# Chunked attention beside a dense expert network: scores in four row tiles, state product in one instruction, state update in column tiles

## The chip, the cores and the metric

One core of one Trainium2 chip, everything in fp32. The metric is the device time of one execution in microseconds (us).

## The reference, cut to what matters

A state-space attention over 4 sequences of 768 tokens with 8 heads (head size 32, state size 16), then a network of 4 experts (256 to 1024 to 256) over all 3072 tokens, weighted by gates.

```python
for c in range(nc):                       # chunks of one sequence
    M = einsum('bhin,bhjn->bhij', Cc, Bc) * L            # scores times decay
    y = einsum('bhij,bhjd->bhid', M, xc)                 # outputs within the chunk
      + einsum('bhin,bhnd->bhid', Cc, state) * decay_to_i  # state product
    state = decay_full * state + sum(Bc x xc * decay_from_j)  # state update
for e in range(E):
    out += p[:, e] * (maximum(x @ w1[e], 0) @ w2[e])
```

The kernel uses chunks of 128 tokens: 24 chunks, six a sequence.

## The kernel before

The expert network runs in 48 steps, each seven first-layer products (`fmul`, into the PSUM banks X and Y, a Strassen-like scheme) and seven second-layer products (`smul`, into four accumulator banks). Chunks 0 to 3 come before step 0. Each of the 20 others is woven into two steps: decays and scores in an even one, outputs and state in the odd one after it. Eight steps make a block of 512 tokens; in the step after a block (step 8, 16 and so on, here a "block end") VectorE and GpSimd combine its accumulators. Between the layers VectorE makes z from X's and Y's products, then h and the differences hT of the second layer ("subtractions" below). Eight PSUM banks are all in use: two for attention ("att"), X, Y, and four accumulators.

```python
def decays(c):                     # VectorE scans, then GpSimd
    LT  = scan(...)                # decay between tokens, by head
    bdec = B * LT[:, :, P-1:P]     # GpSimd reads LT's last column
    cts  = C * dec                 # GpSimd
def scores(c):
    for r in range(2):             # two row tiles of 64, 512 columns each
        k = slice(64 * r, 64 * r + 64)
        g = ps_att.tile([P, NH // 2, P], FP32, tag="att")
        nc.tensor.matmul(out=g, lhsT=xb[k, OBT:OBT + P], rhs=ctm[k], tile_position=(64 * r, 0))
def masked(c):                     # VectorE, in place: LT = g * LT
    for r in range(2): nc.vector.tensor_mul(LT[:, h], g[r], LT[:, h])
def added(c, ...):                 # state update: one product of 256 columns
    nc.tensor.matmul(out=A, lhsT=bdec, rhs=xb[:, 0:DM])
def outputs(c, ...):
    for t in range(NT):            # state product: two of 128 columns
        nc.tensor.matmul(out=y[:, t], lhsT=S[:, t], rhs=cts)
    ...                            # eight outputs, column tiles of 32
# one step n of the loop (cut):
load_weights(n + 2); sum_weights(n + 2)      # GpSimd adds up weights, steps 0 to 5 only
fmul 1, 2; decays(c); smul 1; fmul 6; masks(c); smul 3   # smul: those of step n - 1
outputs(c); added(c)                         # odd steps
fmul 5, 7; smul 7, 5; carry(c); smul 6; fmul 3, 4; combine 0, 1   # combine: block ends only
scores(c); smul 2, 4; masked(c)
```

`masked` overwrites LT, so it has to wait until GpSimd's bdec has read LT. GpSimd takes its work in order, and in steps 0 to 5 bdec stands behind the eight weight sums of that step.

Of the kernel before, what the change touches and what calls it, by code (L numbers as in the profile page):

```python
# [8 lines left out]
FP32 = mybir.dt.float32  # L9
AF = mybir.ActivationFunctionType  # L10
ALU = mybir.AluOpType

P = 128
NQ, NT = 4, 2
# [3 lines left out]
def kernel(  # L18
# [32 lines left out]
    nc = tc.nc  # L51

    NCH, _, W = xbc.shape
    E, DM, F = w1.shape
    NH = NQ * NT
    HN = P
    BLK = 512
    HB = BLK // 2
# [3 lines left out]
    OB, OBT, OCT = DM, DM + HN, DM + 2 * HN  # L62
# [107 lines left out]
    tmask = const.tile([P, NT], FP32, name="tmask")  # L170
    nc.vector.memset(tmask, 0.0)

    smask = const.tile([P, NT, P], FP32, name="smask")
    nc.vector.memset(smask, 0.0)
    for q in range(NQ):
        r = slice(32 * q, 32 * q + 32)
        nc.vector.memset(tmask[32 * q:32 * q + N, 0:1], 1.0)
        nc.vector.memset(smask[r, :, r], 1.0)
    nc.vector.tensor_scalar(out=tmask[:, 1:2], in0=tmask[:, 0:1], scalar1=-1.0, scalar2=1.0,
                            op0=ALU.mult, op1=ALU.add)  # L180
    for t in range(NT):
        nc.vector.tensor_scalar_mul(smask[:, t], smask[:, t], tmask[:, t:t + 1])

    cmask = const.tile([P, NQ // 2, NT], FP32, name="cmask")
    nc.vector.memset(cmask, 0.0)
    for q in range(NQ):
        r = slice(32 * q, 32 * q + 32)
        nc.vector.tensor_copy(cmask[r, q % 2], tmask[r])

    def clip(v):  # L190
        nc.vector.tensor_scalar(out=v, in0=v, scalar1=1e-6, scalar2=1.0, op0=ALU.max, op1=ALU.min)
# [33 lines left out]
    def decays(c):  # L225
        s = st[c]
        if c < DIRECT:
            clip(s["ab"])
            nc.vector.memset(s["ab"].rearrange("p (h s) -> p h s", h=NH)[:, :, 0:1], 0.0)

        LT = att.tile([P, NH * P], FP32, tag="LT", name="LT")
        nc.vector.tensor_tensor_scan(  # L232
            out=LT, data0=s["ab"], data1=ident.rearrange("p h s -> p (h s)"), initial=0.0,
            op0=ALU.mult, op1=ALU.add)
        s["LT"] = LT.rearrange("p (h s) -> p h s", h=NH)

        if c < DIRECT:
            clip(s["ah"])

        s["dec"] = dec = att.tile([HN, P], FP32, tag="dec", name="dec")  # L240
        nc.vector.tensor_tensor_scan(
            out=dec, data0=s["ah"], data1=zeros, initial=1.0, op0=ALU.mult, op1=ALU.add)
        s["bdec"] = bdec = att.tile([P, NH, N], FP32, tag="bdec", name="bdec")
        nc.gpsimd.tensor_mul(  # L244
            bdec, s["xb"][:, OB:OB + HN].rearrange("p (h n) -> p h n", h=NH),
            s["LT"][:, :, P - 1:P].to_broadcast([P, NH, N]))
        s["cts"] = cts = att.tile([HN, P], FP32, tag="cts", name="cts")
        nc.gpsimd.tensor_mul(cts, s["xb"][:, OCT:OCT + P], dec)

    def masks(c):  # L250

        s = st[c]
        m = s["ctm"] = att.tile([P, NQ // 2, NT, P], FP32, tag="ctm", name="ctm")
        for q in range(NQ // 2):
            for t in range(NT):
                nc.scalar.mul(m[:, q, t], s["xb"][:, OCT:OCT + P], cmask[:, q, t:t + 1])  # L256

    def scores(c):
        s = st[c]
        s["g"] = []  # L260
        for r in range(2):
            k = slice(64 * r, 64 * r + 64)
            g = ps_att.tile([P, NH // 2, P], FP32, tag="att", name="g")
            nc.tensor.matmul(  # L264
                out=g.rearrange("p h s -> p (h s)"), lhsT=s["xb"][k, OBT:OBT + P],
                rhs=s["ctm"][k].rearrange("p q t s -> p (q t s)"),
                start=True, stop=True, tile_position=(64 * r, 0))
            s["g"].append(g)

    def masked(c):  # L270
        s = st[c]
        for r in range(2):
            h = slice(NH // 2 * r, NH // 2 * r + NH // 2)
            nc.vector.tensor_mul(s["LT"][:, h], s["g"][r], s["LT"][:, h])  # L274

    state = {}

    def added(c, pool, tag):

        s = st[c]  # L280
        if c % chunks_per_seq < chunks_per_seq - 1:
            A = s["A"] = pool.tile([HN, NT, P], FP32, tag=tag, name="A")
            nc.tensor.matmul(  # L283
                out=A.rearrange("p t m -> p (t m)"), lhsT=s["bdec"].rearrange("p h n -> p (h n)"),
                rhs=s["xb"][:, 0:DM], start=True, stop=True)

    def outputs(c, pool, tag):
        s = st[c]
        first = c % chunks_per_seq == 0
        xb, MT = s["xb"], s["LT"]  # L290
        y = pool.tile([P, NT, P], FP32, tag=tag, name="y")
        if not first:
            for t in range(NT):
                nc.tensor.matmul(out=y[:, t], lhsT=state["S"][:, t], rhs=s["cts"],  # L294
                                 start=(t == 0), stop=False, skip_group_check=True)
        for t in range(NT):
            for q in range(NQ):
                h = NQ * t + q
                nc.tensor.matmul(  # L299
                    out=y[32 * q:32 * q + 32, t], lhsT=xb[:, h * D:h * D + D],  # L300
                    rhs=MT[:, NT * q + t], start=(first and t == 0), stop=True,
                    tile_position=(0, 32 * q), skip_group_check=True)
        k, i = divmod(c, CPB)
        if i == 0:
            yT[k] = ffn.tile([P, NT, BLK], FP32, tag="yT", name="yT")
        nc.scalar.copy(out=yT[k][:, :, i * P:i * P + P], in_=y)

    def carry(c):
        s = st.pop(c)
        if "A" not in s:  # L310
            return
        S = att.tile([HN, NT, P], FP32, tag="S", name="S")
        nc.vector.tensor_mul(S, s["A"], smask)
        if c % chunks_per_seq:
            nc.vector.scalar_tensor_tensor(
                out=S, in0=state["S"], scalar=s["dec"][:, P - 1:P], in1=S,
                op0=ALU.mult, op1=ALU.add)
        state["S"] = S

    def sums(k):  # L320

# [49 lines left out]
    def diff(n, o, x, y):  # L371
        h = hid[n]
        h[o] = ffn.tile([P, JJ, HB], FP32, tag="h" + o, name="h" + o)
        nc.vector.tensor_sub(h[o], h[x], h[y])  # L374
# [3 lines left out]
    def smul(n, i):  # L378

        if n < 0:  # L380
            return
        k = n // SPB
        u, half = divmod(ORDER.index(i), 2)
        if n % SPB == 0 and half == 0:
            acc[k, u] = ps_s.tile([P, 2, HB], FP32, tag=f"acc{u}", name=f"acc{u}")
        w = (A11, A12, S4, A22, S1, S2, S3)[i - 1]
        rhs = hid[n][("11", "21", "22", "T4", "T1", "T2", "T3")[i - 1]]
        for j in range(JJ):
            nc.tensor.matmul(  # L389
                out=acc[k, u][:, half], lhsT=w2_op(n, w)[:, j], rhs=rhs[:, j],  # L390
                start=(n % SPB == 0 and half == 0 and j == 0),
                stop=(n % SPB == SPB - 1 and j == JJ - 1), skip_group_check=True)
# [39 lines left out]

    for c in range(CPB):
        masks(c)
        scores(c)
        decays(c)
        added(c, ps_f, "X")
        masked(c)
        outputs(c, ps_f, "Y")
        carry(c)  # L440
        if c == 0:
            load_decays(1, nc.sync)
            sum_weights(0)
        if c == 1:
            gates()
            sum_weights(1)
        if c == 2:
            load_gate(0, 0)
        load_chunk(c + 2)
# [3 lines left out]
    for n in range(NS + 1):  # L453
# [6 lines left out]
        if run:  # L460
# [9 lines left out]
            total(n, 1, "11")  # L470
            gated(n, "11", "z11")
        if more and not odd:
            decays(c)
        if r == 1 and k > 0:
            leave(k - 1, 0, BLK, both)
        smul(n - 1, 1)
        if run:
            fmul(n, 6)
            snap(n, 6)
        if more and not odd:  # L480
            masks(c)
        smul(n - 1, 3)
        if ending:
            keep(k - 1, 0)
# [14 lines left out]
        if more and odd:  # L499
            carry(c)  # L500
            if c + 2 < NCH:
                load_chunk(c + 2)
        smul(n - 1, 6)
        if ending and not run:
            combine(k - 1, 0, nc.vector)
            combine(k - 1, 1, nc.vector)
            leave(k - 1, HB, HB, (nc.sync, nc.scalar))
        if run:
            fmul(n, 3)
            total(n, 6, "12")  # L510
            fmul(n, 4)
            gated(n, "21", "X")
            gated(n, "12", "z12")
            if more and r == SPB - 1:
                sums(k + 1)
            if ending:
                combine(k - 1, 0, nc.gpsimd)
                combine(k - 1, 1, nc.gpsimd)
            diff(n, "T3", "22", "12")
            diff(n, "T1", "12", "11")  # L520
        if more and not odd:
            scores(c)
        smul(n - 1, 2)
        smul(n - 1, 4)
        if run:
            diff(n, "T2", "22", "T1")
            diff(n, "T4", "21", "T2")
        if more and not odd:
            masked(c)
        if ending:  # L530
            combine(k - 1, 2, nc.vector)
            if not run:
# [46 lines left out]
```

## Time and profile before

Time before: 696.34 us, median of 3 runs (695.63 to 697.55). What each part of a chunk costs on TensorE, and the lines it is read from, stand in the prediction below. "Cost" there and here is the distance from the start of one group of matmuls to the next one's.

An fp32 matmul shows as two records. Starts are used because a matmul's end is modelled: the durations in the lines (1.03 for a group that costs 0.86) contain the drain that overlaps the next group. In a timeline line the columns are start, duration, engine, source line, operation, output and inputs, shapes, number of records, and in brackets the idle time before it with what ended it.

### The profile page before, as it was taken

Reading aid. Unit: us, or ns where it says so; the run is one execution under the profiler, and the core shown is the slowest. Engines: PE = TensorE matmul, PEld = TensorE weight load, DVE = VectorE, ACT = ScalarE, POOL = GpSimd, SP = SyncE. Lnnn points to the kernel's source line nnn. Section 1 sums busy time; section 2 is a strip of 40 time slices with the busy share of each in tenths; the row PEclk is TensorE's granted clock in tenths of the full one; section 3 lists DMA queues with packets and bytes.
Section 4 is the critical chain, followed back from the end, with each engine's and each line's share of the span. In section 5 each row is a group of like instructions: output and inputs, shape, how many; then the busy total and the mean of one; then the engine's idle time right before and its main releaser. Section 6 shows DMA issues by size and latency. Waiting matters only on the chain.

```text
span 695.9 us, 8664 instructions
## 1 busy us (share of the span) xinstructions
PE 661.2 (95%) x3289; PEld 548.2 (79%) x3289; DVE 498.5 (72%) x742; ACT 129.7 (19%) x278; POOL 110.4 (16%) x161
## 2 busy tenths in 40 slices
PE   3588999999999999999999999999999999999995
PEld 1367888887888887888887888887888888788884
DVE  5785867777865868767669858658877685765754
ACT  2120221221221112212212211212122121111110
POOL 5645847002000003000003000000200000200000
PEclk9998999999999999999999999999999999999999
DMA  8778578745655463665455664653673453563301
GB/s 295 285 240 313 171 261 296 279 151 137 237 216 174 140 236 116 205 213 210 137 177 178 174 235 159 227 174 120 181 271 125 130 208 116 142 207 135 106 1 30
DMA packets 71481, 128.89 MB, mean 185 GB/s; under 512 B 29072, under 2 KB 53008, under 8 KB 71440
## 3 DMA queue, kind: packets, MB, share of 16 engines
q1 hardware_dynamic: 66232, 112.93, 48.5%
q0 software_dynamic: 2304, 14.68, 5.3%
q10 hardware_dynamic: 2904, 0.72, 0.5%
q8 instruction: 26, 0.43, 0.3%
q14 instruction: 15, 0.12, 0.1%
HBM read 110.25 MB, written 18.07 MB: 184 GB/s over the span
## 4 chain that ended last, share of the span: by engine, by line
PE 85%; DVE 6%; POOL 1%; DMA 1%; issue 1%; SPq 0%; DVEq 0%; POOLq 0%
PE acc L389 39%; PE X L345 22%; PE Y L345 17%; PE g L264 2%; DVE h L367 2%; PE y L299 2%; PE A L283 2%; DVE hT L374 1%; DMA wt<-in_w_dram 1%; PE y L294 1%; DVE z L357 0%; DVE LT L232 0%; DVE u L409 0%; DVE yS L326 0%; POOL wt L145 0%
## 5 line engine op out<-in xcount | busy, mean ns | idle before, releaser
L357 DVE TENSOR_TENSOR z<-Y,snap 128x512 f32<-128x512 f32 x144 | 98.9, 687 | 158.3 <-ACT snap L352 106.9
L389 PE MATMUL acc<-hT,wt 128*128 128x256 f32 x768 | 181.4, 379 | 0.0
L352 ACT COPY snap<-X 128x512 f32<-128x512 f32 x144 | 84.3, 585 | 482.6 <-PE X L345 474.6
L389 PEld LDWEIGHTS acc<-hT,wt 128*128 128x128 f32 x768 | 146.0, 190 | 19.9
L389 PE MATMUL acc<-h,wt 128*128 128x256 f32 x576 | 149.9, 383 | 4.9 <-DVE u L409 4.9
L345 PE MATMUL X<-yS,wt 128*128 128x256 f32 x576 | 148.6, 381 | 0.0
L389 PEld LDWEIGHTS acc<-h,wt 128*128 128x128 f32 x576 | 107.7, 190 | 34.2 <-issue 11.4
L345 PEld LDWEIGHTS X<-yS,wt 128*128 128x128 f32 x576 | 109.9, 191 | 15.3 <-ACT snap L352 0.2
L367 DVE SCALAR_TENSOR_TENSOR h<-z,gate 128x512 f32<-128x512 f32 x144 | 101.4, 704 | 3.3
L345 PE MATMUL Y<-yT,wt 128*128 128x256 f32 x384 | 98.7, 379 | 1.8 <-DVE z L357 1.8
L345 PEld LDWEIGHTS Y<-yT,wt 128*128 128x128 f32 x384 | 72.9, 190 | 12.1 <-DVE z L357 2.2
L244 POOL TENSOR_TENSOR bdec<-xb,LT 128x128 f32<-128x128 f32 x24 | 10.3, 430 | 408.3 <-PE X L345 264.3
L374 DVE TENSOR_TENSOR hT<-h,hT 128x512 f32<-128x512 f32 x96 | 71.8, 748 | 3.3
L374 DVE TENSOR_TENSOR hT<-h,h 128x512 f32<-128x512 f32 x96 | 67.1, 740 | 1.3
L232 DVE TENSOR_TENSOR_SCAN LT<-ab,ident 128x1024 f32<-128x1024 f32 x24 | 55.9, 2328 | 4.1 <-DMA ab<-acut_d 3.9
L345 PE MATMUL Y<-yS,wt 128*128 128x256 f32 x192 | 51.2, 390 | 0.3
L345 PE MATMUL X<-yT,wt 128*128 128x256 f32 x192 | 49.5, 380 | 0.0
L264 PE MATMUL g<-ctm,xb 64*128 64x512 f32 x96 | 30.9, 724 | 13.8 <-ACT ctm L256 13.8
L345 PEld LDWEIGHTS Y<-yS,wt 128*128 128x128 f32 x192 | 36.2, 193 | 8.1 <-DVE z L357 2.6
L345 PEld LDWEIGHTS X<-yT,wt 128*128 128x128 f32 x192 | 36.3, 190 | 5.8 <-DVE h L367 0.8
L367 DVE SCALAR_TENSOR_TENSOR h<-X,gate 128x512 f32<-128x512 f32 x48 | 33.2, 691 | 8.3 <-PE X L345 8.3
L274 DVE TENSOR_TENSOR LT<-g,LT 128x512 f32<-128x512 f32 x48 | 30.7, 681 | 7.1 <-POOL bdec L244 4.0
(66 smaller groups left out, 298.2 us busy)
## 6 DMA issues: line engine op xcount, KB each, us to landing
wt<-w_d SPq DMA_DIRECT2D x80, 896.0 KB, 4.9
w_d<-wt POOLq DMA_DIRECT2D x16, 896.0 KB, 7.7
ab<-acut_d SPq DMA_DIRECT2D x23, 512.0 KB, 8.2
wt<-in_w_dram SPq DMA_DIRECT2D x32, 256.0 KB, 4.2
xb<-in_xbc_dram SPq DMA_DIRECT2D x24, 320.0 KB, 7.2
gate<-p_d SPq DMA_DIRECT2D x24, 256.0 KB, 6.8
out_dram<-ot SPq DMA_DIRECT2D x40, 64.0 KB, 2.0
ah<-ac_d SPq DMA_DIRECT2D x23, 64.0 KB
```

The lines of the kernel that those rows point to most:

```text
L232: nc.vector.tensor_tensor_scan(out=LT, data0=s["ab"], data1=ident.rearrange("p h s -> p (h s)"), initial=0.0, op0=ALU.mult, op1=ALU.add)
L244: nc.gpsimd.tensor_mul(bdec, s["xb"][:, OB:OB + HN].rearrange("p (h n) -> p h n", h=NH), s["LT"][:, :, P - 1:P].to_broadcast([P, NH, N]))
L264: nc.tensor.matmul(out=g.rearrange("p h s -> p (h s)"), lhsT=s["xb"][k, OBT:OBT + P], rhs=s["ctm"][k].rearrange("p q t s -> p (q t s)"), s ...
L274: nc.vector.tensor_mul(s["LT"][:, h], s["g"][r], s["LT"][:, h])
L283: nc.tensor.matmul(out=A.rearrange("p t m -> p (t m)"), lhsT=s["bdec"].rearrange("p h n -> p (h n)"), rhs=s["xb"][:, 0:DM], start=True, st ...
L299: nc.tensor.matmul(out=y[32 * q:32 * q + 32, t], lhsT=xb[:, h * D:h * D + D], rhs=MT[:, NT * q + t], start=(first and t == 0), stop=True, ...
L345: nc.tensor.matmul(out=f[bank][:, j], lhsT=wt1[n][:, w, j * P:j * P + P], rhs=rhs, start=(i in (1, 2, 5) and j == 0), stop=(j == JJ - 1), ...
L352: nc.scalar.copy(out=s, in_=first[n]["X"])
L357: nc.vector.tensor_add(z, first[n]["Y"], first[n][i])
L367: nc.vector.scalar_tensor_tensor(out=h, in0=first[n][src], scalar=0.0, in1=g.unsqueeze(1).to_broadcast([P, JJ, HB]), op0=ALU.max, op1=ALU. ...
L374: nc.vector.tensor_sub(h[o], h[x], h[y])
L389: nc.tensor.matmul(out=acc[k, u][:, half], lhsT=w2_op(n, w)[:, j], rhs=rhs[:, j], start=(n % SPB == 0 and half == 0 and j == 0), stop=(n % ...
```

## The change

Intent: use more of the array at once in the small attention products. Scores in four row tiles of 32, each in a PSUM bank of its own, so X and Y are borrowed for two of them (before step 0, where four chunks are done in a row, the four accumulator banks are). The state product as one of 256 columns, with C masked instead of the state. The state update in four column tiles, only the blocks that are needed. To free X and Y in time the order of a step changes too: product 6 moves behind the last first-layer product, the scores move behind product 2, and VectorE takes X's and Y's scores first.

```diff
-        for r in range(2):
-            k = slice(64 * r, 64 * r + 64)
-            g = ps_att.tile([P, NH // 2, P], FP32, tag="att", name="g")
+        for q, (pool, tag) in enumerate(homes):
+            k = slice(32 * q, 32 * q + 32)
+            g = pool.tile([P, NT, P], FP32, tag=tag, name="g")
 ...
-            A = s["A"] = pool.tile([HN, NT, P], FP32, tag=tag, name="A")
-            nc.tensor.matmul(out=A..., lhsT=s["bdec"]..., rhs=s["xb"][:, 0:DM], ...)
+            for q in range(NQ):
+                nc.tensor.matmul(out=A[32 * q:32 * q + 32], lhsT=bdec[:, 32 * q:32 * q + 32],
+                    rhs=x[:, q], start=True, stop=True, tile_position=(0, 32 * q))
 ...
-            for t in range(NT):
-                nc.tensor.matmul(out=y[:, t], lhsT=state["S"][:, t], rhs=s["cts"], ...)
+            nc.tensor.matmul(out=y, lhsT=state["M"], rhs=s["cts"], start=True, stop=False, ...)
 ...   (masks: two ScalarE products a chunk, not four; cts on GpSimd twice as wide;
 ...    carry on VectorE: three operations of 32 columns and one of 128)
-        smul(n - 1, 6)
         if run:
             fmul(n, 3) ... fmul(n, 4) ... gated(n, "21", "X") ... gated(n, "12", "z12")
+        smul(n - 1, 6)
+        if ending: combine(k - 1, 0, nc.vector) ...
             diff(n, "T3", "22", "12")
-            diff(n, "T1", "12", "11")
-        scores(c)
-        smul(n - 1, 2)
-        smul(n - 1, 4)
+        smul(n - 1, 2)
+        scores(c, ((ps_att, "att"), (ps_att, "att"), (ps_f, "X"), (ps_f, "Y")))
+        masked(c, (2, 3, 0, 1))
+        smul(n - 1, 4)
+        diff(n, "T1", "12", "11")
             diff(n, "T2", "22", "T1"); diff(n, "T4", "21", "T2")
-        masked(c)
```

More of the change, by code (lines that the diff above doesn't have):

```diff
@@ L171 @@
     nc.vector.memset(tmask, 0.0)
-    smask = const.tile([P, NT, P], FP32, name="smask")
-    nc.vector.memset(smask, 0.0)
+    qmask = const.tile([P, NQ, D], FP32, name="qmask")
+    nc.vector.memset(qmask, 0.0)
     for q in range(NQ):
@@ L177 @@
         nc.vector.memset(tmask[32 * q:32 * q + N, 0:1], 1.0)
-        nc.vector.memset(smask[r, :, r], 1.0)
+        nc.vector.memset(qmask[r, q], 1.0)
     nc.vector.tensor_scalar(out=tmask[:, 1:2], in0=tmask[:, 0:1], scalar1=-1.0, scalar2=1.0,
                             op0=ALU.mult, op1=ALU.add)
-    for t in range(NT):
-        nc.vector.tensor_scalar_mul(smask[:, t], smask[:, t], tmask[:, t:t + 1])
-    cmask = const.tile([P, NQ // 2, NT], FP32, name="cmask")
-    nc.vector.memset(cmask, 0.0)
-    for q in range(NQ):
-        r = slice(32 * q, 32 * q + 32)
-        nc.vector.tensor_copy(cmask[r, q % 2], tmask[r])
     def clip(v):
@@ L246, in decays, with scores, masked @@
             s["LT"][:, :, P - 1:P].to_broadcast([P, NH, N]))
-        s["cts"] = cts = att.tile([HN, P], FP32, tag="cts", name="cts")
-        nc.gpsimd.tensor_mul(cts, s["xb"][:, OCT:OCT + P], dec)
+        s["cts"] = cts = att.tile([HN, NT, P], FP32, tag="cts", name="cts")
+        nc.gpsimd.tensor_mul(cts, s["ctm"], dec.unsqueeze(1).to_broadcast([HN, NT, P]))
     def masks(c):
         s = st[c]
-        m = s["ctm"] = att.tile([P, NQ // 2, NT, P], FP32, tag="ctm", name="ctm")
-        for q in range(NQ // 2):
-            for t in range(NT):
-                nc.scalar.mul(m[:, q, t], s["xb"][:, OCT:OCT + P], cmask[:, q, t:t + 1])
-    def scores(c):
+        m = s["ctm"] = att.tile([HN, NT, P], FP32, tag="ctm", name="ctm")
+        for t in range(NT):
+            nc.scalar.mul(m[:, t], s["xb"][:, OCT:OCT + P], tmask[:, t:t + 1])
+    def scores(c, homes):
         s = st[c]
         s["g"] = []
-        for r in range(2):
-            k = slice(64 * r, 64 * r + 64)
-            g = ps_att.tile([P, NH // 2, P], FP32, tag="att", name="g")
+        for q, (pool, tag) in enumerate(homes):
+            k = slice(32 * q, 32 * q + 32)
+            g = pool.tile([P, NT, P], FP32, tag=tag, name="g")
             nc.tensor.matmul(
-                out=g.rearrange("p h s -> p (h s)"), lhsT=s["xb"][k, OBT:OBT + P],
-                rhs=s["ctm"][k].rearrange("p q t s -> p (q t s)"),
-                start=True, stop=True, tile_position=(64 * r, 0))
+                out=g.rearrange("p t s -> p (t s)"), lhsT=s["xb"][k, OBT:OBT + P],
+                rhs=s["ctm"][k].rearrange("p t s -> p (t s)"),
+                start=True, stop=True, tile_position=(32 * q, 0))
             s["g"].append(g)
-    def masked(c):
+    def masked(c, qs):
         s = st[c]
-        for r in range(2):
-            h = slice(NH // 2 * r, NH // 2 * r + NH // 2)
-            nc.vector.tensor_mul(s["LT"][:, h], s["g"][r], s["LT"][:, h])
+        for q in qs:
+            h = slice(NT * q, NT * q + NT)
+            nc.vector.tensor_mul(s["LT"][:, h], s["g"][q], s["LT"][:, h])
     state = {}
@@ L281, in added @@
         if c % chunks_per_seq < chunks_per_seq - 1:
-            A = s["A"] = pool.tile([HN, NT, P], FP32, tag=tag, name="A")
-            nc.tensor.matmul(
-                out=A.rearrange("p t m -> p (t m)"), lhsT=s["bdec"].rearrange("p h n -> p (h n)"),
-                rhs=s["xb"][:, 0:DM], start=True, stop=True)
+            A = s["A"] = pool.tile([HN, NT, D], FP32, tag=tag, name="A")
+            x = s["xb"][:, 0:DM].rearrange("p (t q d) -> p q t d", t=NT, q=NQ)
+            for q in range(NQ):
+                nc.tensor.matmul(
+                    out=A[32 * q:32 * q + 32],
+                    lhsT=s["bdec"].rearrange("p h n -> p (h n)")[:, 32 * q:32 * q + 32],
+                    rhs=x[:, q], start=True, stop=True, tile_position=(0, 32 * q))
     def outputs(c, pool, tag):
@@ L292, in outputs @@
         if not first:
-            for t in range(NT):
-                nc.tensor.matmul(out=y[:, t], lhsT=state["S"][:, t], rhs=s["cts"],
-                                 start=(t == 0), stop=False, skip_group_check=True)
+            nc.tensor.matmul(
+                out=y.rearrange("p t s -> p (t s)"), lhsT=state["M"].rearrange("p q d -> p (q d)"),
+                rhs=s["cts"].rearrange("p t s -> p (t s)"), start=True, stop=False,
+                skip_group_check=True)
         for t in range(NT):
@@ L311, in carry @@
             return
-        S = att.tile([HN, NT, P], FP32, tag="S", name="S")
-        nc.vector.tensor_mul(S, s["A"], smask)
+        A = s["A"]
+        S = att.tile([HN, NT, D], FP32, tag="S", name="S")
+        nc.vector.tensor_scalar_mul(S[:, 0], A[:, 0], tmask[:, 0:1])
         if c % chunks_per_seq:
             nc.vector.scalar_tensor_tensor(
-                out=S, in0=state["S"], scalar=s["dec"][:, P - 1:P], in1=S,
+                out=S[:, 0], in0=state["S"][:, 1], scalar=s["dec"][:, P - 1:P], in1=S[:, 0],
                 op0=ALU.mult, op1=ALU.add)
-        state["S"] = S
+        nc.vector.scalar_tensor_tensor(
+            out=S[:, 1], in0=A[:, 1], scalar=tmask[:, 1:2], in1=S[:, 0],
+            op0=ALU.mult, op1=ALU.add)
+        M = att.tile([HN, NQ, D], FP32, tag="M", name="M")
+        nc.vector.tensor_mul(M, S[:, 1:2].to_broadcast([HN, NQ, D]), qmask)
+        state["S"], state["M"] = S, M
     def sums(k):
@@ L434 @@
         masks(c)
-        scores(c)
+        scores(c, [(ps_s, f"acc{q}") for q in range(NQ)])
         decays(c)
         added(c, ps_f, "X")
-        masked(c)
+        masked(c, range(NQ))
         outputs(c, ps_f, "Y")
@@ L472 @@
         if more and not odd:
+            masks(c)
             decays(c)
@@ L479 @@
             snap(n, 6)
-        if more and not odd:
-            masks(c)
         smul(n - 1, 3)
@@ L502 @@
                 load_chunk(c + 2)
-        smul(n - 1, 6)
-        if ending and not run:
-            combine(k - 1, 0, nc.vector)
-            combine(k - 1, 1, nc.vector)
-            leave(k - 1, HB, HB, (nc.sync, nc.scalar))
         if run:
@@ L515 @@
                 sums(k + 1)
-            if ending:
-                combine(k - 1, 0, nc.gpsimd)
-                combine(k - 1, 1, nc.gpsimd)
+        smul(n - 1, 6)
+        if ending:
+            combine(k - 1, 0, nc.vector)
+            combine(k - 1, 1, nc.gpsimd if run else nc.vector)
+            if not run:
+                leave(k - 1, HB, HB, (nc.sync, nc.scalar))
+        if run:
             diff(n, "T3", "22", "12")
-            diff(n, "T1", "12", "11")
+        smul(n - 1, 2)
         if more and not odd:
-            scores(c)
-        smul(n - 1, 2)
+            scores(c, ((ps_att, "att"), (ps_att, "att"), (ps_f, "X"), (ps_f, "Y")))
+            masked(c, (2, 3, 0, 1))
         smul(n - 1, 4)
         if run:
+            diff(n, "T1", "12", "11")
             diff(n, "T2", "22", "T1")
             diff(n, "T4", "21", "T2")
-        if more and not odd:
-            masked(c)
         if ending:
```

## The prediction

> **What bounds the kernel now.** I read the page first: the busy line, then the chain that ended last.
>
> ```profile
> PE 661.2 (95%) x3289; PEld 548.2 (79%) x3289; DVE 498.5 (72%) x742; ACT 129.7 (19%) x278; POOL 110.4 (16%) x161
> PE 85%; DVE 6%; POOL 1%; DMA 1%; issue 1%; SPq 0%; DVEq 0%; POOLq 0%
> ```
>
> TensorE is the bound: 95% busy, 85% of the chain. VectorE at 72% has room on average. Next the chain in order of time, to see what a step costs (48 steps of the expert network, two of which carry one of 20 attention chunks; the first 4 chunks come before step 0).
>
> ```profile
> 305.63 2.59 PE acc L389 x12
> 317.71 2.59 PE acc L389 x12
> 332.70 2.59 PE acc L389 x12
> 344.79 2.59 PE acc L389 x12
> ```
>
> The same three products of successive steps: 12.08 us without attention work in between, 14.99 with a chunk's work between, 12.09 again. The plain step is 56 records at 0.216 us (12.09), so TensorE streams without a hole, and a full chunk costs 14.99 - 12.09 = 2.90 us of TensorE. This says that nearly everything the change saves on TensorE there comes off the time. The timeline of TensorE for one such pair of steps splits the 2.90:
>
> ```profile
> 321.00 1.03 PE L345 MATMUL X<-yS,wt 128*128 128x256 f32 x4
> 321.96 1.13 PE L264 MATMUL g<-ctm,xb 64*128 64x512 f32 x4
> 323.02 1.13 PE L389 MATMUL acc<-h,wt 128*128 128x256 f32 x4
> 323.99 1.03 PE L389 MATMUL acc<-hT,wt 128*128 128x256 f32 x4
> ...
> 329.17 0.61 PE L294 MATMUL y<-cts,S 128*128 128x128 f32 x4
> 329.70 0.64 PE L299 MATMUL y<-LT,xb 128*32 128x128 f32 x16
> 330.28 0.70 PE L283 MATMUL A<-xb,bdec 128*128 128x256 f32 x2
> 330.81 1.03 PE L345 MATMUL Y<-yS,wt 128*128 128x256 f32 x4
> 331.68 1.03 PE L345 MATMUL X<-yS,wt 128*128 128x256 f32 x4
> ```
>
> I read starts, since ends are modelled and overlap. A group of 4 ordinary records takes 0.86. The group before the scores takes 0.96, the scores 1.06, the group after them 0.97: together 1.06 + 0.10 + 0.11 = 1.27 for the scores. State product 0.53, outputs 0.58, state update 0.53. Sum 2.91, as above. The matmuls are fp32, two records each.
>
> **Where it is not a pure stream.** The timeline of the early steps, where GpSimd is still summing weights:
>
> ```profile
> 46.81 1.13 PE L264 MATMUL g<-ctm,xb 64*128 64x512 f32 x4
> 47.87 1.13 PE L345 MATMUL X<-yT,wt 128*128 128x256 f32 x4
> 47.97 1.18 POOL L144 TENSOR_TENSOR wt<-wt 128x256 f32<-128x256 f32 x1
> ...
> 53.64 0.42 POOL L244 TENSOR_TENSOR bdec<-xb,LT 128x128 f32<-128x128 f32 x1
> ...
> 54.10 1.29 DVE L274 TENSOR_TENSOR LT<-g,LT 128x512 f32<-128x512 f32 x2 [0.99 <-POOL bdec L244]
> ...
> 54.94 1.19 PE L294 MATMUL y<-cts,S 128*128 128x128 f32 x4 [2.48 <-DVE LT L274]
> ```
>
> The scores of step 0 are ready near 47.9, but VectorE may only multiply them into LT after GpSimd has read LT's last column (bdec), and bdec stands behind the weight sums until 53.64. Today only the outputs at 54.94 wait for that; the next step's X product starts at 47.87 untroubled. And one place at each block's end:
>
> ```profile
> 266.56 1.03 PE L345 MATMUL X<-yS,wt 128*128 128x256 f32 x4
> 267.52 1.13 PE L264 MATMUL g<-ctm,xb 64*128 64x512 f32 x4
> 269.31 1.13 PE L389 MATMUL acc<-h,wt 128*128 128x256 f32 x4 [0.66 <-DVE u L409]
> ```
>
> There the scores partly fill a wait for VectorE's combine.
>
> **What the Trainium skill says.** TensorEngine Tiling (Array Packing), Key Properties: changing the tiling mode drains TensorE. The trace agrees: about 0.10 us more on each side of the scores, and 0.10 on leaving the column-tiled outputs. Same page, Gotcha 1: row tiles must go to different PSUM banks; hence four banks, two of them X and Y. TensorE: Matmul & The Clock Gate, Part 1: after an idle window of some 3.4 us the clock halves and needs as much busy time to recover. The trace has the halving even after 2.48 us of waiting: the groups at 58.09 and 59.80 take 1.71 and 1.61 instead of 0.86. GPSIMD Engine Reference, Specifications: its SBUF interfaces contend with VectorE instructions with two SBUF inputs. Trace: a weight sum is 0.72 us alone and 1.05 to 1.18 beside VectorE's hT subtractions.
>
> **The change, part by part.**
>
> Scores: two row tiles of 64 with 512 columns become four of 32 with 256. Today's 1.06 is two passes of 512 columns at 0.43 (two tiles at once) plus 0.20. Four tiles at once are two passes at 0.216, so 0.43 + 0.20; the switches stay. Saved 0.43 a chunk. Of 20 chunks, one is in the disturbed step 0 and four in block-end steps (below): 15 x 0.43 = 6.5 us.
>
> State product: 4 records of 128 columns become 2 of 256: the same 512 columns. 0.53 is 0.43 of streaming plus the 0.10 switch into column tiling, which stays. Saved 0.
>
> State update: 2 records of 256 columns over the full array become 8 of 64 in four column tiles. Before: 0.43 + 0.10 for the switch back. After: it follows the outputs in the same mode. Streaming is two passes of 64 columns, 0.11; but the outputs' 16 records went by at 0.43/16 = 27 ns each, and I take that as the pace of short records: 8 x 27 ns = 0.22, plus the switch 0.10. Saved 0.53 - 0.32 = 0.21; 16 of the 20 chunks have an update: 3.4 us.
>
> Block ends: product 6 of the second layer moves behind the last first-layer product. In the four block ends with scores, 1.79 (267.52 to 269.31) was scores plus wait. Now product 6 (0.86) fills the 1.89 from the X group's nominal end (267.42) to 269.31, leaving 1.03 idle, then scores without cover: about nothing gained. In the last block end but one, without scores, the wait shrinks by 0.86. In all five the first-layer Y product lost 0.32 to a late z (a group of 1.09, then 0.97); earlier X ends take it away, though the third product now has one group less of slack before it and may give it back. Together 0.9 to 2.5, I take 1.7.
>
> Other engines: masked scores are 4 x 0.42 (the 128x256 from PSUM is 417 ns in the state group) instead of 2 x 0.68: +0.3. State: 2 large operations (0.42 + 0.48) become 3 of 32 columns and one of 128, an estimate of 0.7. ScalarE: 2 mask multiplications less, 0.39 each. GpSimd: cts doubles, 0.49 to about 0.9. All beside TensorE in the steady part; before step 0 the second cts delays the weight sums: +0.3.
>
> X and Y as homes of scores: in a steady step the X product of the next step stands one group (0.86) after the scores. VectorE has finished h21, h12 and T3 by then (3.0 us after the last X product starts, the scores end at 3.4), takes bank X first (0.42, to about 4.0), and X is wanted at 4.4. No wait. But in steps 0, 2 and 4 bdec is late. Step 0: bdec ends 54.06 before. VectorE now stands still instead of running its subtractions, so four weight sums go from 1.05-1.18 to 0.72-0.8: bdec about 1.5 earlier, 52.5; X free at 53.0. Five groups must then run: 4.3 us, plus 1.9 to 3.2 for a cold clock after 5 us idle, then state, outputs, update 1.35: the Y product that started at 58.09 starts about 61, but warm (it lost 1.6 to the cold clock before). Lost 1.5. Step 2: bdec ended at 81.58, X would be wanted near 81.2: with 0.42 for the bank and earlier sums, 0.4. Step 4: bdec ended at 109.36, X wanted near 107.8: about 1.3.
>
> Sum: -6.5 - 3.4 - 1.7 + 0.3 + 1.5 + 0.4 + 1.3 = -8.1. 696.3 - 8.1 = 688.2; I say 688.
>
> **The rivals.** (1) Streaming pays in full and the early steps cost nothing, because the sums finish earlier than I think: 684 to 685. For: the X wait in step 2 is within a fraction of a us. Against: in step 0 bdec is over 4 us late. (2) The new X wait becomes the story: cold clock after each of three waits (today 2.48 us was enough for it), each giving back 2 to 3 us: 692 to 696, perhaps "nothing gained". For: the cold clock in the trace; against: 1.83 us of waiting at 43 to 45 us left the next groups at 0.97. (3) The third product of each step, one group earlier, waits for VectorE's z in every step: at 316.69 the second-last X product starts, z22 ends at 319.06, and the third product would be due at 316.69 + 2.59 = 319.28. The slack is 0.2; if it is gone, 48 x 0.1 to 0.3 is 5 to 14 us: 693 to 702. (4) Four row tiles do not overlap fully: each chunk saves 0.2 less, 4 us: 692.
>
> **Range and chances.** The gains are measured terms (8 to 13); the losses (0 to 9) are guesses of order. 684 to 694 should hold it 8 times in 10. 2% faster is 682.4, below rival 1: 0.07. Slower by 2% is 710, beyond rival 3: 0.02. Within: 0.91.
>
> **What would show it.** Scores at 0.6 to 0.65 between starts instead of 1.06; state update 0.2 to 0.3; the steady pair of steps 26.4 instead of 27.08. In step 0, X waits for VectorE's masked LT for some 5 us with a clock near half behind it; short X waits near 80 and 107. Third Y product: a z wait in most steps would prove rival 3. If the four scores take 0.8 or more, rival 4. I am wrong if steady steps gain under 0.4, or if early steps lose over 6 us.

## The result, and the profile after

688.79 us, median of 4 runs (688.62 to 690.81), against 695.99 before (695.47 to 697.55, 4 runs): ratio 0.990, 95% interval 0.9875 to 0.9924. Ratios here and below are the mean time of one kernel's runs over that of the other's of the same rounds, so they are not quite the ratio of the quoted medians. Predicted: 688, within 684 to 694. The interval of 0.75 to 1.25% lies wholly below the 2% mark. All outputs are right.

The page of the changed kernel, its busy line and its chain by engine:

```profile
PE 644.4 (94%) x3465; PEld 539.0 (78%) x3465; DVE 500.4 (73%) x823; ACT 116.1 (17%) x230; POOL 112.4 (16%) x161
PE 88%; DVE 3%; DMA 2%; POOL 1%; issue 0%; SPq 0%; DVEq 0%; POOLq 0%
```

TensorE lost 17 us of busy time, and the time fell by 7 to 9: not all of the saving arrived. Where it did, the timeline of the changed kernel shows it (the pair of steps that answers to 321 to 332 us before):

```profile
320.83 1.03 PE L392 MATMUL acc<-h,wt 128*128 128x256 f32 x4
321.78 0.71 PE L256 MATMUL g<-ctm,xb 32*128 32x256 f32 x8
322.43 1.13 PE L392 MATMUL acc<-hT,wt 128*128 128x256 f32 x4
322.64 1.42 DVE L266 TENSOR_TENSOR LT<-g,LT 128x256 f32<-128x256 f32 x4 [0.47 <-PE g L256]
323.39 1.03 PE L348 MATMUL X<-yT,wt 128*128 128x256 f32 x4
...
327.71 0.59 PE L288 MATMUL y<-cts,M 128*128 128x256 f32 x2
328.24 0.64 PE L295 MATMUL y<-LT,xb 128*32 128x128 f32 x16
328.70 0.29 PE L277 MATMUL A<-xb,bdec 128*32 128x64 f32 x8
328.92 1.13 PE L348 MATMUL Y<-yS,wt 128*128 128x256 f32 x4
329.89 1.03 PE L348 MATMUL X<-yS,wt 128*128 128x256 f32 x4
```

The scores cost 0.65 (321.78 to 322.43) instead of 1.06. State product 0.53, as before. Outputs and update together 0.68 (328.24 to 328.92) plus 0.11 on the group after, 0.79; before it was 0.58 + 0.53 = 1.11. X starts at 323.39, exactly 0.96 after the group before it: no wait, though VectorE began on the scores only at 322.64.

Where it did not, in the early steps:

```profile
49.04 0.70 PE L256 MATMUL g<-ctm,xb 32*128 32x256 f32 x4 [0.15 <-DVE h L370]
...
53.85 0.42 POOL L236 TENSOR_TENSOR bdec<-xb,LT 128x128 f32<-128x128 f32 x1
54.31 1.42 DVE L266 TENSOR_TENSOR LT<-g,LT 128x256 f32<-128x256 f32 x4 [3.60 <-POOL bdec L236]
54.79 2.07 PE L348 MATMUL X<-yT,wt 128*128 128x256 f32 x4 [5.05 <-DVE LT L266]
56.66 1.84 PE L348 MATMUL Y<-yT,wt 128*128 128x256 f32 x4
...
111.39 1.13 PE L348 MATMUL X<-yT,wt 128*128 128x256 f32 x4 [1.61 <-DVE LT L266]
```

The scores of step 0 are done near 49.7, bdec ends at 54.27, VectorE multiplies, and only then X is free: 5.05 us of idle TensorE. The two groups after it start 1.87 and 1.68 apart instead of 0.86: the clock has halved. X waited another 1.61 us at 111.39, in step 4.

Step 0 also opens at half pace, before any scores of its own. Its first two products, after and then before:

```profile
38.02 2.07 PE L348 MATMUL X<-yT,wt 128*128 128x256 f32 x4
39.89 1.70 PE L348 MATMUL Y<-yT,wt 128*128 128x256 f32 x4
```

```profile
38.21 1.13 PE L345 MATMUL X<-yT,wt 128*128 128x256 f32 x4
39.17 1.03 PE L345 MATMUL Y<-yT,wt 128*128 128x256 f32 x4
```

The third product starts at 41.42 and at 40.04, so the two cost 3.40 us after and 1.83 before. In the one profile that each kernel has, the nine kernels with four-tile scores before step 0 (the changed one and runs 1, 4, 5 and 8 to 12) take 2.36 to 3.57 for these two products, and the five with two-tile scores 1.83 to 2.00. Why the full pace comes back later is not shown by any run.

The same by steps. A step's length is the distance between its first X product and the next step's, read from TensorE's timeline in each profile:

| profile | start of step 0 | steps 0 and 1 | steps 2 to 5 | steps 6 to 47 with the tail |
|---|---|---|---|---|
| before | 38.21 | 29.24 | 53.27 | 575.15 |
| after | 38.02 | 31.99 | 54.44 | 562.49 |
| difference | -0.19 | +2.75 | +1.17 | -12.66 |

From step 6 on the change is worth 12.7 us. The early steps take back 3.7. Of the 2.75 in steps 0 and 1, 1.57 lie in the opening of step 0, and 1.18 behind the start of its scores (21.83 us from there to step 2, against 20.64).

### The profile page after: what moved, and what is told of

The parts are those of the page before. It is cut to its first block, busy times and chain, and to the rows that moved or that the text cites. A ratio compares the mean times of both kernels' runs of the same rounds, so it can differ in the third digit from the quotient of the medians.

```text
span 687.0 us, 9082 instructions
## 1 busy us (share of the span) xinstructions
PE 644.4 (94%) x3465; PEld 539.0 (78%) x3465; DVE 500.4 (73%) x823; ACT 116.1 (17%) x230; POOL 112.4 (16%) x161
## 4 chain that ended last, share of the span: by engine, by line
PE 88%; DVE 3%; DMA 2%; POOL 1%; issue 0%; SPq 0%; DVEq 0%; POOLq 0%
PE acc L392 41%; PE X L348 24%; PE Y L348 18%; DMA wt<-in_w_dram 2%; PE g L256 2%; PE y L295 2%; DVE h L370 1%; PE y L288 1%; DVE LT L224 1%; DVE LT L266 0%; DVE u L412 0%; POOL wt L145 0%; POOL wt L144 0%; PE A L277 0%; POOL wt L146 0%
## 5 line engine op out<-in xcount | busy, mean ns | idle before, releaser
L392 PE MATMUL acc<-hT,wt 128*128 128x256 f32 x768 | 191.1, 382 | 0.0
L392 PEld LDWEIGHTS acc<-hT,wt 128*128 128x128 f32 x768 | 144.3, 190 | 25.2 <-issue 6.3
L392 PE MATMUL acc<-h,wt 128*128 128x256 f32 x576 | 148.3, 380 | 4.9 <-DVE u L412 4.9
L348 PE MATMUL Y<-yT,wt 128*128 128x256 f32 x384 | 100.2, 384 | 2.0 <-DVE z L360 2.0
L377 DVE TENSOR_TENSOR hT<-h,hT 128x512 f32<-128x512 f32 x96 | 68.9, 718 | 3.3
L377 DVE TENSOR_TENSOR hT<-h,h 128x512 f32<-128x512 f32 x96 | 65.0, 701 | 1.3
L348 PE MATMUL X<-yT,wt 128*128 128x256 f32 x192 | 51.5, 392 | 6.7 <-DVE LT L266 6.7
L266 DVE TENSOR_TENSOR LT<-g,LT 128x256 f32<-128x256 f32 x96 | 34.0, 416 | 20.9 <-PE g L256 12.3
L348 PEld LDWEIGHTS Y<-yS,wt 128*128 128x128 f32 x192 | 34.7, 189 | 6.5 <-issue 0.8
L256 PE MATMUL g<-ctm,xb 32*128 32x256 f32 x192 | 19.9, 473 | 11.6 <-ACT ctm L247 11.5
```

The lines of the kernel that those rows point to most:

```text
L256: nc.tensor.matmul(out=g.rearrange("p t s -> p (t s)"), lhsT=s["xb"][k, OBT:OBT + P], rhs=s["ctm"][k].rearrange("p t s -> p (t s)"), start ...
L266: nc.vector.tensor_mul(s["LT"][:, h], s["g"][q], s["LT"][:, h])
L348: nc.tensor.matmul(out=f[bank][:, j], lhsT=wt1[n][:, w, j * P:j * P + P], rhs=rhs, start=(i in (1, 2, 5) and j == 0), stop=(j == JJ - 1), ...
L377: nc.vector.tensor_sub(h[o], h[x], h[y])
L392: nc.tensor.matmul(out=acc[k, u][:, half], lhsT=w2_op(n, w)[:, j], rhs=rhs[:, j], start=(n % SPB == 0 and half == 0 and j == 0), stop=(n % ...
```

## The experiments

In each profile a step's difference from its neighbour kernel can be read to 0.01 us from step 6 on; before that, steps vary with the clock and with when bdec is done.

**1. Weight sums behind bdec, in the changed kernel.** The theory: a late bdec holds bank X, now a home of scores. So let GpSimd do bdec first.

```diff
             load_weights(n + 2)
-            sum_weights(n + 2)
 ...
         decays(c)
+    if run and n + 2 < NS:
+        sum_weights(n + 2)
```

> The changed kernel with one thing moved: in each step GpSimd sums the weights of two steps ahead after the chunk's bdec and cts, not before them. Theory (bank X, now a home of scores, is held by a late bdec): the X waits of 5.0 us in step 0 and 1.6 us in step 4 vanish, and with the first the cold clock behind it (1.8 us); steps 0 and 1 together fall from 32.0 to about 24.2 us and step 4 from 14.7 to about 12.95: some 9 us less, 680 us. Rival (the early steps lose because the prologue ends later and the clock is in another phase, or the weights come late): the waits move to another releaser and the time stays at 687 or above.

Measured: 682.61 us (681.78 to 684.46), ratio to before 0.9805 (0.9784 to 0.9825). Step 4 went from 14.70 to 12.93 as expected, its X wait was gone. Steps 0 and 1 came to 27.91, not 24.2: a shorter X wait stayed in step 0, and the slow clock with it; the opening at half pace (2.93 us for two products) stayed too.

```profile
51.80 2.07 PE L348 MATMUL X<-yT,wt 128*128 128x256 f32 x4 [1.70 <-DVE LT L266]
53.67 1.57 PE L348 MATMUL Y<-yT,wt 128*128 128x256 f32 x4
```

The reason of the wait is in the order of the step: in step 0 there is no previous step, so products 6, 2 and 4 of the second layer are missing, and with them the 2.6 us in which VectorE otherwise gets to the scores. The theory holds in direction; 6.2 us of the expected 9 came.

**2. The same move in the kernel before.**

```diff
             load_weights(n + 2)
-            sum_weights(n + 2)
 ...
         decays(c)
+    if run and n + 2 < NS:
+        sum_weights(n + 2)
```

> The kernel before with the same move of the weight sums. Here no scores lie in X, so only the wait of the outputs of 2.5 us in step 1 and the cold clock behind it (3.1 us) can go: about 5.5 us less, 690.5 us. Together with the run of the changed kernel with this move it tells the change's worth without the early wait: theory, 10 to 11 us instead of 7.2. Rival (the early waits cost both kernels alike): again about 7.

Measured: 694.55 (693.72 to 696.44), ratio 0.9976 (0.9956 to 0.9997). Step 1 fell by 3.9, but in this profile step 0 began 1.2 later, and little was left. Together with run 1, on the same chip and rounds: 0.9805 / 0.9976 = 0.983. With the weight sums out of the way the change is worth 1.7%, some 12 us. By the profiles of runs 1 and 2 this is 12.65 from step 6 on, 1.16 in steps 2 to 5 (where the change lost 1.17 without the move) and 0.55 of an earlier start, less 2.60 in steps 0 and 1 (27.91 against 25.31). So in steps 0 and 1 the early bdec helps both kernels alike, by 4.1 and 3.9 us; what it takes from the change's own loss lies in steps 2 to 5.

**3. The scores alone undone.** Two row tiles of 64 in the attention banks again, all else as changed.

```diff
-        for q, (pool, tag) in enumerate(homes):
-            k = slice(32 * q, 32 * q + 32)
+        for r in range(2):
+            k = slice(64 * r, 64 * r + 64)
+            g = ps_att.tile([P, NH // 2, P], FP32, tag="att", name="g")
```

> The changed kernel with the scores alone undone: two row tiles of 64 with 512 columns in the two attention banks, at the place in the order where the change has them (ScalarE makes both kinds of masked C). Theory: scores 1.06 between starts instead of 0.64, so +0.42 in all 20 chunks, 8.4 us; the X waits in steps 0 and 4 go, but step 1's outputs wait for bdec again as before the change, which leaves some 3 to 4 us of gain: 693 us. Rival (early loss has nothing to do with the banks): 697.

Measured: 694.5 (693.57 to 695.4), ratio 0.9974. Each chunk step from 6 on grew by 0.41 to 0.42. Steps 0 and 1 took 29.10 us, as in the kernel before (29.24), and not 31.99; the opening was back at 1.83. So the scores' tiling, with the banks it borrows and its place before step 0, is worth 0.42 a chunk and brings the loss of steps 0 and 1. Step 5 took 14.25 us here, against 13.07 in the changed kernel: in step 4 VectorE waited 2.78 us for bdec at the multiplication of the scores, and a Y product then 1.21 for a z behind it in VectorE's queue, though no score lay in X or Y.

**4. VectorE takes the attention banks first.**

```diff
-            masked(c, (2, 3, 0, 1))
+            masked(c, (0, 1, 2, 3))
```

> The changed kernel with VectorE taking the four score banks in the order attention, attention, X, Y instead of X, Y first. Theory (X is due one group after the scores): X is released 0.67 us later, at 1.09 us after VectorE starts on the scores instead of 0.42, against 0.75 when TensorE wants it: 0.3 us of X wait in each steady chunk step and 0.67 more in steps 0 and 4, +5 to 6 us, 694 us. Rival (X has slack, the order is idle): within 0.5 us of the changed kernel.

Measured: 700.29 (698.74 to 701.85), ratio 1.0055 (1.0032 to 1.0078): slower than the kernel before. The list of waits, after and in this run (columns: total us, times, longest):

```profile
PE X L348 <- DVE LT L266: 6.7, 2, 5.0
```

```profile
PE X L348 <- DVE LT L266: 12.6, 20, 6.6
```

X now waits in every one of the 20 chunk steps. In a steady chunk it costs 0.33 in the wait and 0.10 in the group that starts again behind it, which I had not counted; steps 0 to 5 cost another 6.0, of which I had expected 1.3, since TensorE also came out of step 4's longer wait (2.95 us) with the slow clock: its next two groups cost 1.71 and 1.42. The direction is as the theory says, and the one-group slack of X is real but thin.

**5. The state product as two of 128 columns again.**

```diff
-            nc.tensor.matmul(out=y, lhsT=M, rhs=cts, start=True, ...)
+            for t in range(NT):
+                nc.tensor.matmul(out=y[:, t], lhsT=M, rhs=cts[:, t], start=(t == 0), ...)
```

> The changed kernel with the state product as two of 128 columns again. Theory (columns set its time: 512 column passes either way): 0.53 us between starts in both, time within 0.5 us of the changed kernel, 688.8. Rival (one instruction less, one weight load less is worth something): +0.1 us in 17 chunks, 690.5.

Measured: 689.92 (689.27 to 691.6), ratio 0.9906. A steady odd step goes from 13.40 to 13.41. The 1.1 us of the profile lies in steps 0 and 1, where the clock recovered later. One instruction or two makes no difference.

**6. The state update alone, in the kernel before.**

```diff
-            A = s["A"] = pool.tile([HN, NT, P], ...)
-            nc.tensor.matmul(out=A, lhsT=bdec, rhs=xb[:, 0:DM], ...)
+            A = s["A"] = pool.tile([HN, NT, D], ...)
+            for q in range(NQ):
+                nc.tensor.matmul(out=A[32 * q:32 * q + 32], ..., tile_position=(0, 32 * q))
-        nc.vector.tensor_mul(S, s["A"], smask)
+        nc.vector.tensor_mul(S, A broadcast over q, smask)
```

> The kernel before with the state update alone in four column tiles of 32 (the sum is spread over the full state by VectorE through a broadcast read). Theory: outputs and update together go from 1.11 to 0.79 us with the switch back included, 0.32 in 16 chunks: 5.1 us, 690.9. My prediction's own figure, 0.21, would give 692.6. Rival (column tiles cost a drain of their own): no gain, 696.

Measured: 691.55 (688.34 to 693.75), ratio 0.9922 (0.9888 to 0.9955). Each odd step with an update fell by 0.32 exactly, 13.73 to 13.41. My predicted 0.21 is refuted.

**7. Product 6 moved, alone, in the kernel before.**

```diff
-        smul(n - 1, 6)
         if run:
             fmul(n, 3) ... fmul(n, 4) ...
+        smul(n - 1, 6)
+        if ending: combine(k - 1, 0, nc.vector) ...
```

> The kernel before with the second layer's product 6 moved behind the last first-layer product, alone. Theory: the late z at the five block ends goes (0.32 each), the last but one block end waits 0.86 less, and at four block ends product 6 and the scores together cover the wait for VectorE's combine (0.73 each): 1.6 + 0.9 + 2.9 = 5.4 us, 690.6. Rival (the third Y product, one group earlier, now waits for z in every step): no gain or a loss, 696 to 702.

Measured: 691.31 (689.32 to 691.79), ratio 0.9912 (0.9888 to 0.9936). The four block-end steps with scores fell by 1.06 (14.40 to 13.34), the fifth by 1.19, and all other even steps stayed at 13.34. No step shows a new wait of the third Y product: rival 3 of the prediction is refuted. So an order of instructions alone, without any tiling, is worth 5.4 us from step 6 on (575.15 to 569.78). Within the change it brings less: there the scores move behind product 2 too, and the block ends give 4 x 0.35 + 1.19 = 2.6 of the 12.7.

**8. The scores under the combine at block ends, with run 1's move.** After the change the scores stand behind product 2, which at a block end waits for VectorE's combine with nothing over it:

```profile
374.50 1.13 PE L392 MATMUL acc<-h,wt 128*128 128x256 f32 x4 [0.85 <-DVE u L412]
375.56 0.71 PE L256 MATMUL g<-ctm,xb 32*128 32x256 f32 x8
```

```diff
-        smul(n - 1, 2)
+        if not ending: smul(n - 1, 2)
         scores(c, ...); masked(c, (2, 3, 0, 1))
+        if ending: smul(n - 1, 2)
```

> The changed kernel with the weight sums after bdec and cts, and at block ends the scores before product 2, so that they run while VectorE combines. Theory: as the first of these, and at four block ends another 0.74 us: 3.0 us below it, 677 us. Rival (X is not yet read there, or VectorE takes the scores later): no difference from the first.

Measured: 677.72 (676.53 to 679.42), ratio 0.9729 (0.9706 to 0.9751). The four block-end steps fell from 14.05 to 13.21. In this run's timeline the wait that remains is a quarter of it:

```profile
365.94 0.71 PE L256 MATMUL g<-ctm,xb 32*128 32x256 f32 x8
366.86 1.13 PE L392 MATMUL acc<-h,wt 128*128 128x256 f32 x4 [0.21 <-DVE u L412]
```

**9. Other banks for step 0's scores, in the changed kernel.** If X alone carries the late bdec to TensorE, borrowing accumulators 2 and 3 in step 0 should do.

```diff
+            free = ((ps_s, "acc2"), (ps_s, "acc3")) if n == 0 else ((ps_f, "X"), (ps_f, "Y"))
-            scores(c, ((ps_att, "att"), (ps_att, "att"), (ps_f, "X"), (ps_f, "Y")))
+            scores(c, ((ps_att, "att"), (ps_att, "att")) + free)
```

> The changed kernel with one difference: in step 0 alone the third and fourth score tile go to the banks of accumulators 2 and 3, which nothing needs until late in step 1, and not to X and Y. GpSimd's order stays, so bdec is as late as in the changed kernel. Theory (it is the bank that carries the late bdec into the next X product): the X wait of 5 us in step 0 goes; the outputs of step 1 wait for the scores instead, as in the kernel before, some 2 us with a cold clock behind it. Steps 0 and 1 together about 28.5 us instead of 32.0, time 685.3. Rival (the late bdec costs the same wherever the scores lie): 688 to 689.

Measured: 688.95 (688.14 to 690.48), ratio 0.988 (0.986 to 0.99): a miss, no gain over the changed kernel's 0.990 that the intervals separate. The wait moved:

```profile
54.61 1.42 DVE L266 TENSOR_TENSOR LT<-g,LT 128x256 f32<-128x256 f32 x4 [4.42 <-POOL bdec L236]
55.84 0.67 PE L288 MATMUL y<-cts,M 128*128 128x256 f32 x2 [2.84 <-DVE LT L266]
...
59.55 2.07 PE L348 MATMUL Y<-yS,wt 128*128 128x256 f32 x4 [2.35 <-DVE z L360]
```

X started at 48.42 without a wait, but the outputs waited 2.84 and the next Y product 2.35, for a z that stood in VectorE's queue behind the scores' multiplications and the subtractions after them. The change puts `masked` ahead of three subtractions in that queue; while it waits for bdec, VectorE does nothing else. Behind the start of the scores steps 0 and 1 took 22.03 us, against 21.83 in the changed kernel; steps 4 and 5 lost 2.4 (30.14 against 27.77), where X waited 2.29 us instead of 1.61 and the slow clock followed. My theory of the bank alone falls for step 0.

**10. The same banks in the best version.**

```diff
+            free = ((ps_s, "acc2"), (ps_s, "acc3")) if n == 0 else ((ps_f, "X"), (ps_f, "Y"))
-            scores(c, ((ps_att, "att"), (ps_att, "att"), (ps_f, "X"), (ps_f, "Y")))
+            scores(c, ((ps_att, "att"), (ps_att, "att")) + free)
```

> The kernel with the later weight sums and the scores under the block-end combine, and with the same two accumulator banks in step 0. Its step 0 had still 2.6 us of waiting for X and a cold clock behind it, since step 0 has no second-layer products between the scores and the next X product. Theory: step 0 falls from 13.55 to about 10.3 us and step 1 from 15.2 to about 13.4: 5 us, 673 us. Rival (the cold clock of step 1 comes from the 1.8 us wait for z earlier in step 0, not from the wait for X): step 0 gains 2.6 and step 1 nothing, 675.

Measured: 676.51 (675.66 to 677.79), ratio 0.9707 (0.9689 to 0.9725); run 8's interval overlaps. In the profiles step 0 gained 3.5 and step 1 only 0.4: the Y product behind the update waited 1.18 us for VectorE's z. Of these 3.9, 1.06 is a shorter opening of step 0, which the edit does not touch; behind the start of the scores the two steps fell from 18.45 to 15.61. That is below the 16.71 of the kernel before with the same early bdec (run 2): with bdec early and other banks, the loss behind the scores is gone. It is the fastest kernel measured, by a margin over run 8 that is not clear.

**11 and 12. Bank and queue, the other two corners.** Run 11 takes run 9's banks and, in step 0, lets VectorE multiply the scores after the subtractions, as before the change. Run 12 does only the latter.

```diff
-            masked(c, (2, 3, 0, 1))
+            if n: masked(c, (2, 3, 0, 1))
 ...
             diff(n, "T4", "21", "T2")
+        if n == 0: masked(c, (2, 3, 0, 1))
```

> The run with accumulator banks in step 0 gained nothing: the wait moved from X to the outputs (2.8 us) and to the next Y product (2.4 us), whose z stood in VectorE's queue behind the scores' multiplications and three subtractions. So here both: accumulator banks in step 0, and in step 0 VectorE multiplies the scores after the subtractions, as in the kernel before. Theory (bank and VectorE's queue each carry the late bdec to TensorE, and either is enough): steps 0 and 1 together as in the kernel before less the scores' and update's gain, about 28.5 us instead of 32.0; 685.3 us. Rival (the early loss is in neither: clock phase and weights): 688 to 689.

> The fourth corner: the changed kernel's banks, X and Y, but in step 0 VectorE multiplies the scores after the subtractions. Theory: X is still held by the late bdec, and the subtractions running beside the weight sums make these slower again, so steps 0 and 1 stay at 31.5 to 32.5 us, time within 1 us of 688.8. Rival (VectorE's queue alone carries the loss): about 28.5 us for the two steps, 685.3.

Measured: run 11 689.63 (685.45 to 689.98), ratio 0.988 (0.9843 to 0.9918); run 12 690.06 (689.76 to 690.45), ratio 0.9904. Steps 0 and 1 took, in brackets what came behind the start of step 0's scores (20.64 in the kernel before):

| step 0's scores | multiplied ahead of the subtractions | behind them |
|---|---|---|
| in X and Y | 31.99 [21.83] (the changed kernel) | 33.07 [22.69] (run 12) |
| in the accumulators | 31.69 [22.03] (run 9) | 30.83 [21.71] (run 11) |

Neither part alone helps, and both together hardly do: of run 11's 1.16 us, 1.05 is a shorter opening of step 0, before anything that the edit touches. With bank and queue both out of the way, the outputs wait, as they did in the kernel before (2.48):

```profile
56.32 1.19 PE L288 MATMUL y<-cts,M 128*128 128x256 f32 x2 [4.09 <-DVE LT L266]
```

In run 11 the weight sums began at 45.54 and bdec at 54.63, against 44.67 and 53.64 in the kernel before. That is about one more us, and it belongs to neither bank nor queue. And what run 11 gained, its profile gives back in steps 4 and 5 (30.15 against 27.77): it reached step 4 earlier, X waited 2.30 us there instead of 1.61, and TensorE came out of that wait with the slow clock. One of its four runs took 685.45, the others 689.4 and more; why that one was faster no profile shows. What does help is shown by runs 1 and 10: bdec early, and only then other banks.

## Why the prediction was right

- **Scores, 0.43 a chunk: right.** Measured 0.42 in run 3, and 0.65 between starts where 0.63 was worked out. Rival 4 (tiles that overlap only partly) is refuted.
- **State product, nothing: right.** Run 5.
- **State update, 0.21 a chunk: mis-sized, it is 0.32** (run 6). The step that failed is the switch out of column tiling, part of which was paid twice. The outputs cost 0.46 where a column-tiled update follows and 0.57 where a full-array product does; that product then costs 0.97 instead of 0.86 (chunks without an update show both, in either kernel). The working kept the outputs at 0.58, with their share of the switch, and added 0.22 + 0.10: 0.90 in all, where 0.46 + 0.22 + 0.11 = 0.79 was measured. Whether the update's 0.22 is the pace of 27 ns a record, or two passes of 0.055 and a share of the switch, no run separates. Sixteen chunks at 0.11 make 1.8 us.
- **Block ends, 0.9 to 2.5, taken as 1.7: the upper end came true.** The late z's 0.32 is gone at all five, and at the last 0.87 more (step 40, 14.40 to 13.21). With scores, only 0.35 in all: the uncovered scores gained nothing, as predicted.
- **X and Y as homes in a steady step, no wait: right,** and run 4 shows how thin it is.
- **Early steps, 3.5 lost (0.3 + 1.5 + 0.4 + 1.3): mechanism in part right, size too small.** Counted as the prediction does, without what the early scores and updates save, the profiles give 5.2.
  - The term that failed most is the prologue's 0.3. Step 0 began 0.19 earlier, but it opened at half pace, which cost 1.57. The prediction has no term for that.
  - Step 0's 1.5 came out at 1.5 (1.18 and the 0.32 that the update saves), with some luck. X was free at 54.79 and not at 53.0: the weight sums began at 45.67 instead of 44.67, and bdec then came only 0.79 sooner after their start and not 1.5, because VectorE still ran one subtraction beside them. But the scores came 1.4 later as well, and the clock behind the wait cost 1.8 where 1.9 to 3.2 was allowed. Both sums waited for the weights' DMA; whether it was late because of the doubled cts is not shown.
  - Step 2 had no X wait, but a late z: 0.45 lost where 0.4 was predicted. Step 4 lost 1.8 where 1.3 was predicted, 1.61 of it the X wait. Rival 2's cold clock followed the wait of step 0 alone.
- **That the late bdec costs time through X: not X alone.** Runs 3, 9, 11 and 12 show three ways to TensorE, the bank, VectorE's queue and the outputs, and closing one opens the next.

The total held partly because errors of some 2 us in each direction cancelled: the later steps gave 12.7 where the terms add up to about 10 (measured: scores 5.3, updates 4.6, block ends 2.6), the early ones lost more. What remains open is why step 0 opens at half pace. An early bdec together with other banks in step 0 removes what was lost behind its scores (run 10).

## What to carry to other kernels

Where one engine streams without a hole, price a change by the distances between starts, and count each share of a mode switch once, with the group that pays it. Before a buffer is borrowed, ask for every phase of the program, the first steps above all, which engine releases it and what that engine must wait for first; in an in-order queue a wait for the borrowed buffer stops all that stands behind it. Moving one instruction that blocks can be worth as much as faster tiles: here product 6 alone gave about 0.9%, and bdec ahead of the weight sums took the changed kernel from 0.990 to 0.9805 of the time before. When an edit seems to gain in a step, look whether the gain lies behind the first instruction that the edit touches: in run 11 nearly all of it lay before.

## What the Trainium skill lacked or had wrong

- TensorEngine Tiling (Array Packing), Key Properties, says that a change of the tiling mode drains TensorE and gives no size. Here row-tiled scores add 0.10 us to the group before them and 0.11 to the group after (0.96 and 0.97 for groups that cost 0.86 elsewhere). Leaving column tiles adds 0.11 to the outputs (0.57 instead of 0.46) and 0.11 to the full-array group behind them (0.97).
- TensorE: Matmul & The Clock Gate, Part 1, puts the fall to half the clock after an idle window of some 3.4 us. Here half pace followed waits of 2.48 us (before, at 54.94) and 1.70 us (run 1, at 51.80, with another 1.83 us wait 5 us earlier), and did not follow a single one of 1.61 us (after, at 111.39). A wait shorter than the stated window is no safety.
